# Singles in every odd step, small pieces of ScalarE and VectorE tied to the kind of step, and the output weights rounded on GpSimd

## The chip, the cores and the metric

The kernel runs on one core of one Trainium2 chip. The core has TensorE (matrix products, which go to the accumulation memory PSUM), VectorE, ScalarE and GpSimd, which run side by side and wait for each other by semaphores, and a sync engine, SP, that issues DMAs. The metric is device time of one execution in microseconds, median of the runs shown. The profile abbreviates: PE is TensorE, PEld its weight loads, DVE VectorE, ACT ScalarE, POOL GpSimd. L with a number is a line of the kernel; after a change the same code stands some lines further down.

## The reference

Two attention branches over the same input `x` (2048 rows of 512) are mixed by a gate per row; 32 heads of 16 in both.

```python
x = A_x
g = _sigmoid((x * gate_w).sum(-1, keepdims=True))
a = _A_ref(x, A_wqkv, A_wo)          # 8 keys per row: positions pos - 2*w, w = 0..7
b = _B_ref(x, B_wq, B_wk, B_wv, B_wo)  # all 2048 keys, one k and v for all heads
return g * a + (1 - g) * b
...
scores = jnp.einsum("bhqd,bkd->bhqk", q, k) * (Dh ** -0.5)
p = _softmax(scores, axis=-1)
o = jnp.einsum("bhqk,bkd->bhqd", p, v)
```

Branch A is small per row and runs mostly on GpSimd; branch B is the large one.

## The kernel before

**Front.** Up to about 278 us the projections of both branches run on TensorE (L1138), in float32 split into a rounded high part and a remainder. In between, maxima of branch B's first scores are taken. The change does not reorder anything there.

**Main loop.** Branch B is cut into 32 units `u` (four query blocks of 512 rows by eight groups of four heads) of 16 key blocks, so 512 steps `s`; step `s` is key block `s % 16` of unit `s // 16`. I number steps from 0. In a step TensorE does

- two score pairs (L488, `exp_pair`), each into one of two banks pairs `pe`, from which ScalarE takes an exponential of 128 x 1024 (L494);
- the weighted sum of the step before (L503, `weighted`) into `po`;
- work for a later unit: softmax needs each row's maximum before its exponentials, so scores are multiplied out once more in advance and reduced by VectorE. A *pair* fills two banks `pm` (L344) and costs VectorE one reduction of 128 x 1024 (L366, `fill_pair`); a *single* fills the bank `ps` and costs one of 128 x 512 (L378, `fill_one`). Each step takes a pair; some steps take a single as well.

Which steps take a single is decided by `singles(s)`: `owing` grows every step by the share of the remaining maxima that pairs cannot cover, a single is due when it reaches 1, and it is put off when VectorE is ahead of TensorE on the planner's clock.

**Small pieces.** Between steps stand short instructions for other work, all placed by the same planner, which keeps clocks `clk` for TensorE, ScalarE and VectorE, and `pool` for GpSimd, from estimated durations. `run_tasks` issues what is due by TensorE's clock: `shift_a` (ScalarE, tile `mh`, L458), which begins turning a unit's maxima into two more rows of its queries, and `finish_c` (VectorE, the transpose into `ob`, L543), which shapes two finished units. `run_pool` first runs the `hooks` that are due, `a_max` (VectorE, `amx`, L587), `a_exp` (ScalarE, `lg`, L596) and `a_sum` (VectorE, `asum`, L600), which are branch A's softmax; then it hands GpSimd pieces of branch A from the generator `work` as long as GpSimd's clock is less than 2.5 us ahead. A piece of GpSimd that needs a hook's result is held back until the hook has been issued. At the end of a unit (`kt == 0`) VectorE turns `po` (L517) and takes reciprocals (L523); when the last maximum of a unit is in, `filled` adds a reduction and a small transpose (`ms`, `mt`, L354 and L356).

**Output.** `work` also loads the output weights (`wo_load`, DMA on SP) and splits them (`wo_split`): ScalarE rounds 128 x 512 to `woh` (L81), GpSimd subtracts it for `wol` (L82). One such element of `extra` follows each pair of branch A's groups. After steps 271, 399 and 447 four output rows each are multiplied out in an *output phase* (`out_phase`, L821), in which score maxima go on; it needs the low halves that GpSimd subtracts in `prepare` (L662). Branch A has 32 groups, of which 16 belong to the first half of the rows and must be done before the first phase, the other 16 before the third. The last four output rows end the kernel.

All engines run their instructions in the order in which this program issues them, so the planner's placement is the order on each queue.

Of the kernel before, what the change touches and what calls it, by code (L numbers as in the profile page):

```python
# [48 lines left out]
def gated_mix_kernel(ctx, tc, xt, wa, wk, wq, wo_a, wo_b, out):  # L49
# [272 lines left out]
    hooks, pool, done = [], 0.0, set()  # L322

    marks, ups = [], [0]

    def mark(inst, end, up=None):
        marks.append((ups[0] if up is None else up, end, inst.ins.name))
# [21 lines left out]
    def filled(v, n):  # L349
        left[v] -= n  # L350
        if not left[v]:
            ms = wp.tile([P, 2, 2, 8], F32, name="ms")
            m = mx.pop(v).rearrange("p b i t k -> p b (i t) k")
            nc.vector.tensor_reduce(ms, m.unsqueeze(2).to_broadcast([P, 2, 2, 8, 4]), AX.X, ALU.max)  # L354
            mt = wp.tile([P, 32], F32, name="mt")
            nc.vector.transpose(mt, ms.rearrange("p b x y -> p (b x y)"))  # L356
            if v + 2 < NU:
                unit_tile(v + 2)
            tasks.append((after("dve", 0, 0.66) + (0.1 if pe else 2.0), shift_a, (v, mt)))
# [94 lines left out]
        fill_one(dst, key)  # L454

    def shift_a(v, mt):
        th = wp.tile([P, 32], F32R, name="mh")
        nc.scalar.activation(th, mt, AF.Identity, scale=mk[:, 4:5])  # L458
        at = after("act", 0, 0.25)
        ml = wp.tile([P, 32], F32R, name="ml")  # L460
        tasks.append((at + 0.1, shift_c, (v, mt, th, ml)))
# [74 lines left out]
                finish_c(u, obp["t"])  # L536

    def finish_c(u, t):
        shaped.add(u)
        qb, hg = divmod(u, NHG)  # L540
        if hg == 1:
            ob[qb] = pe[0].tile([P, C, 512], F32, name="ob", bufs=2)
        nc.vector.transpose(ob[qb][:, hg // 2, :], t.rearrange("p b h d -> p (b h d)"))  # L543
        after("dve", 0, 0.7)
        if qb == NQB - 1 and hg < NHG - 1:
            last_parts(hg // 2)
# [83 lines left out]
    p2b = []  # L630
# [18 lines left out]

    def wo_split(k, c):  # L650
        t = wot.pop((k, c))
        split(woh[k][:, c, :], wol[k][:, c, :], t, nc.gpsimd)

    turned, later = {}, {}

# [152 lines left out]

    def out_phase(js, n, s):

        m = 3 * (C + n)
        items = {}

        def mm(b, at):
            x, j, i = at
            if j not in items:
                items[j] = out_items(j, n)
                clk["pe"] = max(clk["pe"], free[f"e{x % 2}"])
            st, mv = items[j][i]
            h = slice(64 * b, 64 * b + 64)  # L820
            nc.tensor.matmul(eb[x % 2][:, b, :], st()[h], mv[h], start=(i == 0), stop=(i == m - 1))  # L821
            return T_R

        def done(at):
            x, j, i = at
            if i % 4 == 3:
                run_tasks()
                run_pool()
            if i == (5 if x else 1):
                turn(j, 1 - x % 2)  # L830
            if i == (8 if x else 6):
                later.pop(j)()
            if i == 3 * n and j != js[-1]:
                prepare(js[x + 1], n)
            if j == js[-1] and i > 9 and s not in exped and (free["e0"] <= clk["pe"] or i == m - 4):
                exp_pair(s, 0)
            if i == m - 1:
                out_store(j, x % 2, j == js[-1])

        stream([(x, j, i) for x, j in enumerate(js) for i in range(m)], mm, done, s)  # L840
# [47 lines left out]
    def singles(s):  # L888

        steps = 16 * (NU - 1) - 8 - s  # L890
        if steps <= 0 or to_go() <= 0:
            return to_go() > 0
        owing[0] += (to_go() - 1.94 * steps - 15.5 * (NJ - 4 - outs)) / steps
        owing[0] = min(owing[0], 3.0)
        if s % 16 == 1:
            return True
        if s % 16 == 0 or owing[0] < 1.0 or clk["dve"] - clk["pe"] > 1.5 and owing[0] < 2.0:
            return False
        return True

    def fill_ready(key, slack):
        if fillable() and free[key] <= clk["pe"] + slack:
# [104 lines left out]
    def work():  # L1007
# [28 lines left out]
        def load(i):  # L1036
            if i < len(order):
                yield lambda: order[i][0] // GC < ready_gg
                a_load(*order[i])
                yield 600 if i else 6200  # L1040

        order = [(g, hf) for hf in range(2) for g in range(NAG)]
        extra, summing = list(wos), []
        yield from load(0)
        yield from load(1)
        for i in range(0, len(order), 2):
            yield from a_scores(*order[i])
            hooks.append((pool + 3500, a_max, order[i][0], ("max",) + order[i]))
            for k, x in enumerate(a_scores(*order[i + 1])):
                yield x  # L1050
                if k == 6:
                    yield from sub(*order[i])
                if k == 11:
                    yield from sums()
            hooks.append((pool + 3500, a_max, order[i + 1][0], ("max",) + order[i + 1]))
            for k, x in enumerate(values(*order[i])):
                yield x
                if k == 6:
                    yield from sub(*order[i + 1])
                if k == 11:  # L1060
                    yield from sums()
            yield from load(i + 2)
            yield from values(*order[i + 1])
            yield from load(i + 3)
            if p2b and extra:
                for f, a in extra.pop(0):
                    f(*a)
                yield 1300
        assert not extra

    pieces, blocked = [work()], []
# [1 line left out]
    def run_pool():  # L1073
        nonlocal pool
        now = clk["pe"] * 1e3
        for h in sorted(hooks, key=lambda h: h[0]):
            if h[0] <= now:
                hooks.remove(h)
                h[1](h[2])
                done.add(h[3])  # L1080
        while pieces and pool < now + 2500:
            if blocked and not blocked[0]():
                break
            blocked.clear()
            x = next(pieces[0], None)
            if x is None:
                pieces.clear()
            elif callable(x):
                blocked.append(x)
            else:  # L1090
                pool = max(pool, now) + x
# [194 lines left out]
    qst.append(pe[0].tile([P, 2, 512], F32R, name="qsty"))  # L1286
    clear(NB + 1, nc.gpsimd)
    outs, due, led = 0, [], set()
    for s in range(NS + 1):
        u, kt = divmod(s, NJ)  # L1290
        if len(stacked) < NU and s >= max(2, 16 * (gone(len(stacked)) + 1)):
# [13 lines left out]
        if s - 1 in led:  # L1305
            order = (0, "m1", 1, "m2", "po")
        k, n = outs // 4, C - (outs >= NJ - 4)
        if outs == NJ - 4:
            if short > 0 and steps < 2:
                pause(short)  # L1310
# [12 lines left out]
        for which in order:  # L1323
            if which == "m2":
                if slots or half:
                    fill_ready("m2", 1.2 if s - 1 in led else M2S)
                else:
                    next(tail, None)
            elif which == "m1":
                if singles(s) and fill_ready("m1", M1S):  # L1330
                    owing[0] -= 1.0
            elif which == "po":
                weighted(s - 1)
            elif s < NS:
                exp_pair(s, which)
        if s - 1 in exped:
            weighted(s - 1)
            if kt == 0 and s < NS:
                finish_a(u - 1, nc.gpsimd)
        run_tasks()  # L1340
        run_pool()
    assert not slots and not half and not hooks and not tasks and first[0] > 12, (len(slots), len(hooks), len(tasks), outs)
# [78 lines left out]
```

## Time and profile before

| what | us |
|---|---|
| median of three runs (1441.04 to 1441.69) | 1441.46 |
| the profiled execution | 1441.69 |
| its span, first to last instruction | 1439.9 |
| TensorE busy | 1430.7 |
| ScalarE busy | 1299.8 |
| VectorE busy | 1120.1 |
| GpSimd busy | 946.9 |
| start of step 0 | 278.1 |
| the three output phases with their first step behind | 38.2, 38.7, 38.5 |

The time lies 1.8 us above the span, which is what surrounds the first and last instruction. The granted TensorE clock was 1.00. Busy time of TensorE says little by itself, since matmuls are pipelined and their ends modelled; starts of matmuls are the better ruler, and a step is measured from the start of its first score pair to that of the next step. In the timeline view a row has start, duration, engine, line, operation, output and inputs, count and, in brackets, how long the engine sat idle before it and for whom.

### The profile page before, as it was taken

The page shows a single profiled execution, that of the slowest core. Times are in us where ns is not written, and L with a number is a line of the kernel's source. Part 1 is how long each engine was busy: PE and PEld are TensorE (multiplying, and loading weights), DVE is VectorE, ACT ScalarE, POOL GpSimd, SP SyncE. Part 2 cuts the span into 40 slices and gives each one's busy share as a digit, 9 for nine tenths or more (in the row PEclk, how much of TensorE's full clock was granted, in tenths as well). Part 3 has the DMA queues.
Part 4 walks back from the last instruction along what each step waited for, and adds up shares of the span by engine and source line. Part 5 has one row for each costly group of instructions (what it writes and reads, how often), then busy time and mean ns, then how long its engine had stood idle before and what let it go on. Part 6 is the DMA issues. An engine that isn't in the chain of part 4 may idle for free.

```text
span 1439.9 us, 29642 instructions
## 1 busy us (share of the span) xinstructions
PE 1430.7 (99%) x10985; PEld 748.2 (52%) x10985; DVE 1120.1 (78%) x1851; ACT 1299.8 (90%) x1679; POOL 946.9 (66%) x1708
## 2 busy tenths in 40 slices
PE   9999999999999999999999999999999999999999
PEld 6999999833333333333333374333333743373335
DVE  7888899878787887887877777878778777777721
ACT  6888888799999999999999989999999889979994
POOL 6831989887889889888898898888883310140010
PEclk9999999999999999999999999999999999999999
DMA  7653342421211202012021120211200000000000
GB/s 237 179 165 111 114 135 74 129 64 39 80 43 49 79 13 79 32 39 69 13 80 45 40 88 18 81 43 43 72 12 13 17 16 1 2 31 2 1 2 30
DMA packets 45689, 85.51 MB, mean 59 GB/s; under 512 B 10400, under 2 KB 28376, under 8 KB 41448
## 3 DMA queue, kind: packets, MB, share of 16 engines
q1 hardware_dynamic: 38552, 45.21, 10.2%
q0 software_dynamic: 6560, 37.95, 8.1%
q8 instruction: 86, 1.41, 0.4%
q14 instruction: 59, 0.48, 0.1%
q10 hardware_dynamic: 432, 0.46, 0.1%
HBM read 57.77 MB, written 25.25 MB: 58 GB/s over the span
## 4 chain that ended last, share of the span: by engine, by line
PE 97%; ACT 1%; issue 1%; DMA 0%; DVE 0%; SPq 0%; ACTq 0%; DVEq 0%
PE po L503 35%; PE pe L488 24%; PE pf L1138 11%; PE pm L344 8%; PE ps L344 5%; PE pe L821 4%; PE pd L415 4%; PE po L344 1%; ACT pexp L494 1%; PE pf L344 1%; PE pe L1350 1%; PE pd L931 0%; DMA xraw<-xt 0%; PE pm L879 0%; PE pf L205 0%
## 5 line engine op out<-in xcount | busy, mean ns | idle before, releaser
L494 ACT ACTIVATE pexp<-pe 128x1024 f32<-128x1024 f32 x1021 | 982.6, 1023 | 51.6 <-PE pe L488 46.1
L366 DVE TENSOR_REDUCE mx<-pm 128x2 f32<-128x1024 f32 x479 | 585.2, 1222 | 193.7 <-PE pm L344 189.7
L503 PE MATMUL po<-pexp,vst 128*32 128x512 f32 x4096 | 545.5, 605 | 0.0
L488 PE MATMUL pe<-qst,kst 64*128 64x512 f32 x1914 | 477.1, 460 | 3.8 <-DVE other L704 3.2
L488 PEld LDWEIGHTS pe<-qst,kst 64*128 64x128 f32 x1914 | 185.5, 183 | 452.6 <-ACT pexp L494 413.4
L427 ACT ACTIVATE dd<-pd 128x512 f32<-128x512 f32 x410 | 231.7, 603 | 49.9 <-PE pd L415 39.6
L566 POOL TENSOR_TENSOR pr<-aext 128x256 f32<-128x256 f32 x256 | 182.0, 738 | 4.8 <-DMA aext<-ad 4.6
L344 PE MATMUL pm<-kst,qst 62*128 62x512 f32 x877 | 177.4, 397 | 0.0
L626 POOL TENSOR_TENSOR oa<-oa,av 128x256 f32<-128x256 f32 x224 | 164.1, 733 | 15.5
L378 DVE TENSOR_REDUCE mx<-ps 128x1 f32<-128x512 f32 x246 | 167.2, 680 | 2.6 <-PE pe L821 1.4
L503 PEld LDWEIGHTS po<-pexp,vst 128*32 128x32 f32 x4096 | 80.6, 108 | 158.4 <-issue 149.1
L415 PE MATMUL pd<-kd,qst 62*128 62x512 f32 x405 | 156.9, 395 | 0.0
L344 PE MATMUL ps<-kst,qst 62*128 62x512 f32 x387 | 154.6, 400 | 0.6 <-DVE mx L439 0.6
L623 POOL TENSOR_TENSOR av<-aext,lg 128x256 f32<-128x256 f32 x224 | 139.3, 622 | 13.0
L1138 PE MATMUL pf<-wah,xh 64*128 64x384 f32 (+1 forms) x496 | 144.1, 339 | 0.0
L1138 PE MATMUL pf<-wah,xl 64*128 64x384 f32 (+1 forms) x496 | 141.9, 338 | 0.0
L1138 PE MATMUL pf<-wal,xh 64*128 64x384 f32 (+1 forms) x496 | 141.8, 337 | 0.0
L439 DVE CUSTOM_DVE_ANT_0 dd<-ps,dd 128x512 f32<-128x512 f32 x164 | 113.0, 689 | 29.1 <-PE ps L344 12.4
L439 DVE CUSTOM_DVE_ANT_0 dd<-po,dd 128x512 f32<-128x512 f32 x146 | 100.5, 688 | 11.3 <-PE po L344 4.5
L530 POOL TENSOR_TENSOR rl<-rl,gate_t 128x16 f32<-128x16 f32 x31 | 7.1, 229 | 136.9 <-DVE rl L523 136.8
L1138 PEld LDWEIGHTS pf<-wah,xh 64*128 64x128 f32 x496 | 87.4, 186 | 0.4
L1138 PEld LDWEIGHTS pf<-wal,xh 64*128 64x128 f32 x496 | 87.0, 186 | 0.1
(224 smaller groups left out, 1909.3 us busy)
## 6 DMA issues: line engine op xcount, KB each, us to landing
aext<-ad POOLq DMA_DIRECT2D x32, 1056.0 KB, 5.4
ad<-stage SPq DMA_DIRECT2D x32, 384.0 KB
qst<-qd SPq DMA_DIRECT2D x60, 128.0 KB
xraw<-xt SPq DMA_DIRECT2D x16, 256.0 KB
qd<-qhi SPq DMA_DIRECT2D x16, 256.0 KB
qd<-qlo SPq DMA_DIRECT2D x16, 256.0 KB
qst<-qd SPq DMA_DIRECT2D x60, 64.0 KB
qst<-ml SPq DMA_DIRECT2D x212, 2.0 KB
```

The lines of the kernel that those rows point to most:

```text
L344: nc.tensor.matmul(dst, qst[place(v)][b:b + 62, pr, t * P:(t + 1) * P], kst[b:b + 62, kc * 512:(kc + 1) * 512], start=True, stop=True)
L366: got = nc.vector.tensor_reduce(m[:, :, pr, t, kc], dst, AX.X, ALU.max)
L378: got = nc.vector.tensor_reduce(m[:, odd, pr, t, kc:kc + 1], dst, AX.X, ALU.max)
L415: nc.tensor.matmul(dst, qst[place(v)][b:b + 62, pr, t * P:(t + 1) * P], kd[0][b:b + 62, kc // 2, :], start=True, stop=True)
L427: got = nc.scalar.activation(held[b][k], dst, AF.Relu)
L439: got = nc.vector.tensor_tensor_reduce(held[b][k], dst, held[b][k], 1.0, -FMAX, ALU.add, ALU.max, m[:, b, pr, t, kc:kc + 1])
L488: nc.tensor.matmul(bank[:, odd, :], kst[b:b + 64, kt * P:(kt + 1) * P], qst[place(u)][b:b + 64, pr, :], start=True, stop=True)
L494: got = nc.scalar.activation(e, bank, AF.Exp, scale=SCALE)
L503: nc.tensor.matmul(po[32 * i:32 * i + 32, :], vst[:, kt, :], pexp[s, i // 2][:, i % 2, :], start=(kt == 0), stop=(kt == NJ - 1))
L566: nc.gpsimd.tensor_mul(pr[:, k], q, e[:, o:o + NH, AC:2 * AC])
L626: nc.gpsimd.tensor_add(ao, ao, av)
L1138: inst = nc.tensor.matmul(home(x)[0][:, :n], l[h], r[h], start=(i == 0 and b == 0), stop=(i == 3 * C - 1 and b == 1))
```

## The change

Five edits go together.

1. `singles(s)`: from step 2 of a unit on, an odd step takes a single as long as `owing` is not negative; an even one only when 2 are owing. The first step of a unit takes none and its second always one, as before.
2. `calm(eng)`: in the main loop an engine may issue at most one small piece per step, and none where `quiet` is set. `quiet` is set behind every step: for ScalarE where the step had no single and the one before had, for VectorE where it had a single and the one before had none, and in any case at a unit's first step and where a unit's last maximum came in. A piece that finds its engine quiet is put back by half a microsecond or left in `hooks`.
3. `shift_a`, `finish_c` (but for the last units) and the hooks ask `calm`. In the output phases `main` is false, and nothing is held back there.
4. `wo_split` rounds on GpSimd instead of ScalarE.
5. The elements of `extra` are issued twice per pair of branch A's groups instead of once, and charge GpSimd 2000 ns instead of 1300.

```diff
+    quiet, main, over = {"act": 0, "dve": 0}, [False], []
+
+    def calm(eng):
+        if main[0] and quiet[eng] > 0:
+            return False
+        quiet[eng] = 1
+        return True
...
     def filled(v, n):
         left[v] -= n
         if not left[v]:
+            over.append(v)
...
     def shift_a(v, mt):
+        if not calm("act"):
+            tasks.append((clk["pe"] + 0.5, shift_a, (v, mt)))
+            return
...
     def finish_c(u, t):
+        if u < NU - NHG and not calm("dve"):
+            tasks.append((clk["pe"] + 0.5, finish_c, (u, t)))
+            return
...
     def wo_split(k, c):
         t = wot.pop((k, c))
-        split(woh[k][:, c, :], wol[k][:, c, :], t, nc.gpsimd)
+        nc.gpsimd.tensor_copy(woh[k][:, c, :], t)
+        nc.gpsimd.tensor_sub(wol[k][:, c, :], t, woh[k][:, c, :].bitcast(F32))
...
     def out_phase(js, n, s):
 
+        main[0] = False
...
         if s % 16 == 1:
             return True
-        if s % 16 == 0 or owing[0] < 1.0 or clk["dve"] - clk["pe"] > 1.5 and owing[0] < 2.0:
-            return False
-        return True
+        return s % 16 > 0 and owing[0] >= (0.0 if s % 2 else 2.0)
...
+        def outputs():
+            if p2b and extra:
+                for f, a in extra.pop(0):
+                    f(*a)
+                yield 2000
...
             yield from load(i + 2)
+            yield from outputs()
             yield from values(*order[i + 1])
             yield from load(i + 3)
-            if p2b and extra:
-                for f, a in extra.pop(0):
-                    f(*a)
-                yield 1300
+            yield from outputs()
...
-            if h[0] <= now:
+            if h[0] <= now and calm("act" if h[1] is a_exp else "dve"):
...
+    run, same = 0, 0
     for s in range(NS + 1):
...
+        main[0], lone = True, 0
...
                 if singles(s) and fill_ready("m1", M1S):
                     owing[0] -= 1.0
+                    lone = 1
...
+        run = run + 1 if lone == same else 1
+        same = lone
+        quiet["act"], quiet["dve"] = int(run < 2 and not lone), int(run < 2 and lone or kt == 0 or bool(over))
+        over.clear()
         run_tasks()
         run_pool()
```

TensorE's order over steps 127 to 129 (128 is the first of unit 8). `pe` are the banks of the exponentials, `pm` those of a pair, `ps` that of a single. Before:

```order
L488 MATMUL pe_4339<-qst_83,kst 128x512 x2
L344 MATMUL pm<-kst,qst_79 128x512 x2
L488 MATMUL pe_4340<-qst_83,kst 128x512 x2
L503 MATMUL po<-pexp,vst 32x512 x4
L488 MATMUL pe_4339<-qst_84,kst 128x512 x2
L344 MATMUL pm<-kst,qst_79 128x512 x2
L488 MATMUL pe_4340<-qst_84,kst 128x512 x2
L503 MATMUL po<-pexp,vst 32x512 x4
L488 MATMUL pe_4339<-qst_84,kst 128x512 x2
L344 MATMUL pm<-kst,qst_79 128x512 x2
L344 MATMUL ps<-kst,qst_79 128x512
L488 MATMUL pe_4340<-qst_84,kst 128x512 x2
```

and now:

```order
L500 MATMUL pe_4339<-qst_83,kst 128x512 x2
L352 MATMUL pm<-kst,qst_79 128x512 x2
L352 MATMUL ps<-kst,qst_79 128x512
L500 MATMUL pe_4340<-qst_83,kst 128x512 x2
L515 MATMUL po<-pexp,vst 32x512 x4
L500 MATMUL pe_4339<-qst_84,kst 128x512 x2
L352 MATMUL pm<-kst,qst_79 128x512 x2
L500 MATMUL pe_4340<-qst_84,kst 128x512 x2
L515 MATMUL po<-pexp,vst 32x512 x4
L500 MATMUL pe_4339<-qst_84,kst 128x512 x2
L352 MATMUL pm<-kst,qst_79 128x512 x2
L352 MATMUL ps<-kst,qst_79 128x512
```

Step 127 has a single (`ps`) now, and step 128 without one follows a step with one instead of a step without. Step 129 has its single in both.

ScalarE's order over steps 75 to 77, before (`woh` is a rounding of output weights, behind step 76):

```order
L494 ACTIVATE pexp<-pe_4339 128x1024
L494 ACTIVATE pexp<-pe_4340 128x1024
L494 ACTIVATE pexp<-pe_4339 128x1024
L494 ACTIVATE pexp<-pe_4340 128x1024
L81 ACTIVATE woh_4420<-os 128x512
L494 ACTIVATE pexp<-pe_4339 128x1024
L494 ACTIVATE pexp<-pe_4340 128x1024
```

and now (`lg` is an exponential of branch A, behind step 75, which has a single):

```order
L506 ACTIVATE pexp<-pe_4339 128x1024
L506 ACTIVATE pexp<-pe_4340 128x1024
L611 ACTIVATE lg<-lg 128x128
L506 ACTIVATE pexp<-pe_4339 128x1024
L506 ACTIVATE pexp<-pe_4340 128x1024
L506 ACTIVATE pexp<-pe_4339 128x1024
L506 ACTIVATE pexp<-pe_4340 128x1024
```

The rounding has left ScalarE. GpSimd has it now, ahead of its subtraction, for the first time here, between a load of branch A and its next products:

```order
L641 TENSOR_TENSOR oa<-oa,av 128x8x32
L570 DMA aext<-ad 128x2112
L667 CAST woh_4420<-os 128x512
L668 TENSOR_TENSOR wol_4421<-os,woh_4420 128x512
L581 TENSOR_TENSOR pr<-aext 128x256 x4
L587 TENSOR_TENSOR tr_4908<-pr 128x512
```

Before, only the subtraction stood on GpSimd.

GpSimd's order in the second output phase, from the low half of its first row (`qst<-ob`) to that of the third, before (`mx` is the clearing of a tile of maxima, `two` the sum of two halves of an output row, `rl` and `obp` a finished unit):

```order
L662 TENSOR_TENSOR qst_84<-ob,qst_84 128x512
L530 TENSOR_TENSOR rl<-rl,gate_t 128x16
L531 TENSOR_TENSOR obp<-tt,rl 128x16x16
L662 TENSOR_TENSOR qst_84<-ob,qst_84 128x512
L710 TENSOR_TENSOR two<-two 128x512
L338 MEMSET mx 128x64
L662 TENSOR_TENSOR qst_84<-ob,qst_84 128x512
```

and now, the ten rows that end with the low half of the third row:

```order
L631 TENSOR_TENSOR asum<-asum,gate 128x16
L632 TENSOR_TENSOR lg<-lg,asum 128x128
L638 TENSOR_TENSOR oa_4419<-aext,lg 128x8x32
L638 TENSOR_TENSOR av<-aext,lg 128x256
L726 TENSOR_TENSOR two<-two 128x512
L346 MEMSET mx 128x64
L641 TENSOR_TENSOR oa_4419<-oa_4419,av 128x8x32
L638 TENSOR_TENSOR av<-aext,lg 128x256
L641 TENSOR_TENSOR oa_4419<-oa_4419,av 128x8x32
L678 TENSOR_TENSOR qst_84<-ob,qst_84 128x512
```

Branch A's values (`av`, `oa`) and weights (`lg`, `asum`) stand between the low halves of the second and the third row now; before, branch A had ended ahead of this phase. The phases themselves follow the same steps as before.

## The prediction

> **What bounds the kernel now.** I read the page first, then the row of each stage, then single steps in order of time. The page's first part and its chain:
>
> ```profile
> PE 1430.7 (99%) x10985; PEld 748.2 (52%) x10985; DVE 1120.1 (78%) x1851; ACT 1299.8 (90%) x1679; POOL 946.9 (66%) x1708
> ...
> PE 97%; ACT 1%; issue 1%; DMA 0%; DVE 0%; SPq 0%; ACTq 0%; DVEq 0%
> ```
>
> TensorE carries nearly the whole chain, so a gain has to appear as a shorter stretch between TensorE instructions. The change touches only the 512 attention steps, of which 478 lie outside the three output phases. The windows view, cut at the starts of steps 2, 271, 274, 399, 402, 447, 450 and 489, with the exponentials of L494 alone (length, ScalarE busy, count; two exponentials are one step):
>
> ```profile
> 284.77:832.53 547.76, 517.07 (x538) 1.00 0.16 51
> 870.76:1124.08 253.32, 240.12 (x250) 1.00 0.12 39
> 1162.74:1253.62 90.88, 85.93 (x90) 1.00 0.02 4
> 1292.12:1371.27 79.15, 74.48 (x78) 1.00 0.02 5
> ```
>
> So 956/2 = 478 steps take 971.1 us. The same windows for the tile `ps` give the steps with a single (PE, PEld, DVE with the count of reductions); first and last of the four rows, the others count 60 and 21:
>
> ```profile
> 284.77:832.53 547.76, 54.05 (x136) 25.32 (x136) 92.20 (x137) 0.00 (x0) 1.00 0.16 51
> ...
> 1292.12:1371.27 79.15, 7.65 (x19) 3.53 (x19) 12.92 (x19) 0.00 (x0) 1.00 0.02 5
> ```
>
> 237 singles for 478 steps: half of the steps have one. What does an undisturbed alternation cost? In order of time, the first score matmul of step 184 and that of step 192, between which steps with and without a single alternate and no small piece of ScalarE or VectorE falls:
>
> ```profile
> 655.25 0.50 PE L488 MATMUL pe<-qsty,kst 64*128 64x512 f32 x2
> ...
> 671.31 0.50 PE L488 MATMUL pe<-qst,kst 64*128 64x512 f32 x2
> ```
>
> Eight steps in 16.06 us, 4.015 a pair. 239 such pairs would take 959.6, so 971.1 - 959.6 = 11.5 us of these stages is irregularity. That is the most that ordering can win, and the parts below say how much of it goes.
>
> **Part 1: two steps without a single in a row.** Steps 127 and 128 have none, step 129 has one (starts of steps 127, 128, 129 and 130, and a weight load between):
>
> ```profile
> 539.29 0.50 PE L488 MATMUL pe<-qst,kst 64*128 64x512 f32 x2
> ...
> 541.19 0.50 PE L488 MATMUL pe<-qst,kst 64*128 64x512 f32 x2
> ...
> 541.82 0.19 PEld L488 LDWEIGHTS pe<-qst,kst 64*128 64x128 f32 x2 [0.29 <-ACT pexp L494]
> ...
> 543.25 0.50 PE L488 MATMUL pe<-qst,kst 64*128 64x512 f32 x2
> ...
> 545.38 0.50 PE L488 MATMUL pe<-qst,kst 64*128 64x512 f32 x2
> ```
>
> The first takes 1.90 us, the second 2.06: its second score pair waits for ScalarE to leave bank `pe1`. The step with a single takes 2.13, which is TensorE's own time. So a step without a single is cheap only behind one with: the second in a row pays 0.16 and gets nothing for it. By the order of TensorE's instructions, before has 26 steps that follow another without a single, after has 4 (steps 347, 348, 383, 384). 22 x 0.16 = **3.5 us saved**. Runs of two with a single fall from 22 to 8; that their second step costs more no row quoted here shows, and I take nothing (up to 0.05 each would be 0.7, low end of the range). The planner ends with 239 steps with a single where it had 236: 3 x (2.13 - 1.90) = **0.7 us lost**.
>
> **Part 2: the eight roundings of the output weights leave ScalarE.** Four stand behind a step without a single, four behind one with. One of each (the rounding, then the starts of the steps after it, with a wait):
>
> ```profile
> 437.99 0.63 ACT L81 ACTIVATE woh<-os 128x512 fp32r<-128x512 f32 x1
> ...
> 439.64 0.50 PE L488 MATMUL pe<-qst,kst 64*128 64x512 f32 x2
> ...
> 440.50 0.19 PEld L488 LDWEIGHTS pe<-qst,kst 64*128 64x128 f32 x2 [0.56 <-ACT pexp L494]
> ...
> 441.93 0.50 PE L488 MATMUL pe<-qst,kst 64*128 64x512 f32 x2
> ```
>
> ```profile
> 496.38 0.50 PE L488 MATMUL pe<-qst,kst 64*128 64x512 f32 x2
> ...
> 496.62 0.63 ACT L81 ACTIVATE woh<-os 128x512 fp32r<-128x512 f32 x1
> ...
> 498.56 0.50 PE L488 MATMUL pe<-qst,kst 64*128 64x512 f32 x2
> ...
> 500.55 0.50 PE L488 MATMUL pe<-qst,kst 64*128 64x512 f32 x2
> ```
>
> In the first, the step from 439.64 takes 2.29 instead of 1.90: 0.39 lost, by a TensorE wait for ScalarE. In the second, 2.18 and 1.99 stand for 2.13 and 1.90: 0.14. Together 4 x 0.39 + 4 x 0.14 = **2.1 us saved**. GpSimd takes the casts over. The nearest row is its cast of a tile of the same shape, beside ScalarE's:
>
> ```profile
> L246 POOL CAST qhi<-qraw 128x512 fp32r<-128x512 f32 x13 | 7.9, 611 | 10.7 <-ACT qraw L239 10.7
> ...
> L81 ACT ACTIVATE woh<-os 128x512 fp32r<-128x512 f32 x8 | 5.1, 632 | 0.0
> ```
>
> 8 x 0.61 = 4.9 us more on GpSimd, behind which only its own later branch A pieces stand; what hides it is that no output phase needs them yet (rival C). The loads of the next weights on SP wait for GpSimd's subtraction of the one before, as they did; what is queued behind them on SP are loads of queries for units some steps ahead, so nothing is charged. The Trainium skill, page "Perfetto Trace Analysis", section "Optimizing GPSIMD Operations", says to prefer other engines, since GpSimd is generally slower; the two rows here are 611 against 632 ns, so for this operation the trace does not agree, and the rule would matter only by way of rival C.
>
> **Part 3: small pieces change their steps.** An exponential of branch A behind a step without a single, and the two step starts after it; then VectorE's transpose of `ob` behind a step with one:
>
> ```profile
> 698.58 0.31 ACT L596 ACTIVATE lg<-lg 128x128 f32<-128x128 f32 x1
> ...
> 700.23 0.50 PE L488 MATMUL pe<-qst,kst 64*128 64x512 f32 x2
> ...
> 702.19 0.51 PE L488 MATMUL pe<-qst,kst 64*128 64x512 f32 x2
> ```
>
> ```profile
> 358.54 0.70 DVE L543 STREAM_TRANSPOSE ob<-obp 128x512 f32<-128x512 f32 x1
> ...
> 360.05 0.50 PE L488 MATMUL pe<-qst,kst 64*128 64x512 f32 x2
> ...
> 360.41 0.19 PEld L344 LDWEIGHTS pm<-kst,qsty 62*128 62x128 f32 x2 [0.17 <-DVE mx L366]
> ...
> 362.31 0.50 PE L488 MATMUL pe<-qst,kst 64*128 64x512 f32 x2
> ```
>
> The first costs 1.96 - 1.90 = 0.06, two steps later, when the backlog reaches the bank. The second costs 2.26 - 2.13 = 0.13, because the pair reduction behind it comes late and TensorE waits for `pm`. Of 28 exponentials in these stages 15 stand behind a step without a single, and all but one of them move; 9 transposes stand behind a step with one and all move: 14 x 0.06 + 9 x 0.13 = **2.0 us saved**. In their new places I cost them at nothing: a step with a single gives ScalarE 2.13 - 1.90 = 0.23 more, nearly the 0.31 of a piece, and a step without has no second reduction on VectorE. If that cover is too thin, up to the whole 2.0 stays. The row maxima and reciprocals of branch A (a quarter to a third of a microsecond on VectorE) move too; they are taken at nothing, between -0.5 and +0.5. The new waits are only delays by the planner of at most a few steps; behind them are pieces of GpSimd.
>
> **Sum.** -3.5 + 0.7 - 2.1 - 2.0 = -6.9 us. This leaves 11.5 - 6.9 = 4.6 of irregularity: 4 x 0.16 are known, 0.7 are the added singles, and first steps behind output phases and ends of units remain. The profiled execution took 1441.69 with a span of 1439.9, so 1.8 lie around the span: 1441.69 - 6.9 = 1434.8. The median of the three runs is 0.2 below the profiled one: **1434.6**.
>
> **Rivals.** A: *ScalarE is the bound.* In the rows of the stages it is busy 94 to 95% with exponentials alone. Then regular singles buy nothing and the span loses just the 5.1 us of the `woh` row: 1436.4. Against it: the second step without a single waits for ScalarE, the first does not, and a step with a single is 0.23 longer although ScalarE does nothing more in it. The Trainium skill, "Perfetto Trace Analysis", "Identifying the Most-Contended Engine", says that TensorE's busy share is no measure and that for ScalarE occupancy is; it would point to A, and the step rows speak against it for the alternation.
>
> B: *the pieces only move their lateness.* Parts 1 and 2 hold, part 3 gives nothing: 1441.5 - 3.5 - 2.1 + 0.7 = 1436.6. For it: 0.31 is more than 0.23.
>
> C, the slow side: *GpSimd comes late.* With delays and casts, branch A's last two groups slip from before the second output phase into it. There the `lo` halves of the rows are subtracted on GpSimd with 9 to 12 branch A instructions between them; at the 0.6 to 0.75 us of such an instruction some 7 to 8 us. A row of the phase takes 38.66/4 = 9.7 us and the subtraction is issued half a row ahead, so if a whole group stood ahead of it TensorE would wait up to 3.5 us in each of three rows, and the exponentials of branch A that now fall into the phase (0.31 each) come on top: +11, 1445.6. It decides the sign once more than 6.9 are lost there. The first two output phases (windows; PE, PEld, DVE, ACT, POOL):
>
> ```profile
> 832.53:870.76 38.23, 37.24 (x332) 31.11 (x329) 29.25 (x76) 30.52 (x51) 35.16 (x50) 1.00 0.27 90
> 1124.08:1162.74 38.66, 37.64 (x333) 29.62 (x329) 28.93 (x75) 30.27 (x50) 13.97 (x18) 1.00 0.07 22
> ```
>
> Against it: the first phase already runs with GpSimd 92% busy in branch A and is the shorter one.
>
> D: *no change.* The pieces held back delay GpSimd and VectorE until new waits eat the gain: 1441. Against it: the order shows the alternation really built, with the same three phases at the same steps.
>
> **Chances.** Forecast 0.64, B 0.14, A 0.09, D 0.07, C 0.06. The range reaches down towards the 11.5 of all irregularity (1430.0) and up past A and B with 1 us for the second output phase: 1431.0 to 1438.0, which leaves out C and D. About 0.2% (2.9 us) can be told from no change: faster (below 1438.6) 0.87, within 0.07, slower 0.06.
>
> **What would show it.** The four stages should fall from 971.1 to about 964 us, with steps alternating 1.90 and 2.13; no L81 row of `woh` on ScalarE and a cast near 0.61 on GpSimd; the second phase between 38 and 39.5 with GpSimd near 90%. I am wrong if steps without a single, behind one with, often take more than 1.95, if the second phase passes 42, or if the gain is ScalarE's 5 us and no more.

## The result, and the profile after

The changed kernel takes 1433.12 us (median of five runs, 1432.92 to 1433.91) where the kernel before took 1441.04 (1440.89 to 1441.69) beside it. The ratio is 0.9944, with a 95% interval of 0.9931 to 0.9957: faster by 0.56%. The forecast was 1434.6 in a range of 1431.0 to 1438.0. The profiled execution took 1432.93 us with a span of 1431.2, against 1441.69 and 1439.9.

The page of the changed kernel, busy times and the engines' shares of the chain:

```profile
PE 1422.7 (99%) x10985; PEld 750.6 (52%) x10985; DVE 1121.1 (78%) x1854; ACT 1296.0 (91%) x1671; POOL 949.3 (66%) x1708
...
PE 97%; POOL 2%; ACT 0%; issue 0%; DVE 0%; POOLq 0%; ACTq 0%; DVEq 0%
```

TensorE carries 97% of the chain as before. Its busy time fell by 8.0, about as much as the span (8.7), although it issues the same 10985 matmuls: modelled busy time swallows the short waits, which is why the stages have to be read by starts of steps.

The windows of the four stages between the output phases, with ScalarE's exponentials (now L506; length, ScalarE busy, count), and the first and the last row for the tile `ps` (PE, PEld, DVE with the count of reductions; the two others count 60 and 22):

```profile
284.26:825.91 541.65, 515.25 (x538) 1.00 0.15 47
864.34:1115.68 251.34, 239.09 (x250) 1.00 0.15 48
1154.16:1244.87 90.71, 85.75 (x90) 1.00 0.02 4
1283.47:1362.49 79.02, 74.35 (x78) 1.00 0.02 5
```

```profile
284.26:825.91 541.65, 53.59 (x136) 25.37 (x136) 92.59 (x137) 0.00 (x0) 1.00 0.15 47
...
1283.47:1362.49 79.02, 8.37 (x21) 3.90 (x21) 14.24 (x21) 0.00 (x0) 1.00 0.02 5
```

The same 478 steps take 962.7 us instead of 971.1: 8.4 of the 8.7 us of span were won here. 239 steps in them have a single, as the order had it (the reductions count 240, since one at the edge of a window belongs to the step ahead). The other 0.3 are the front, whose program is the same and which ended 0.5 earlier in this execution, and the phases and the end, 0.2 longer in sum.

The place where the order was shown, steps 126 to 129 in order of time (starts of their first score pairs):

```profile
534.18 0.50 PE L500 MATMUL pe<-qst,kst 64*128 64x512 f32 x2
...
536.08 0.49 PE L500 MATMUL pe<-qst,kst 64*128 64x512 f32 x2
...
538.20 0.50 PE L500 MATMUL pe<-qst,kst 64*128 64x512 f32 x2
...
540.10 0.50 PE L500 MATMUL pe<-qst,kst 64*128 64x512 f32 x2
```

1.90, 2.12, 1.90: step 128, which took 2.06 before, is now a cheap step behind one with a single. An exponential of branch A in its new place, behind the step that starts at 692.81 and has a single, and the three steps after it:

```profile
692.81 0.50 PE L500 MATMUL pe<-qst,kst 64*128 64x512 f32 x2
...
694.95 0.50 PE L500 MATMUL pe<-qst,kst 64*128 64x512 f32 x2
695.18 0.31 ACT L611 ACTIVATE lg<-lg 128x128 f32<-128x128 f32 x1
...
696.84 0.50 PE L500 MATMUL pe<-qst,kst 64*128 64x512 f32 x2
...
698.97 0.50 PE L500 MATMUL pe<-qst,kst 64*128 64x512 f32 x2
...
700.87 0.50 PE L500 MATMUL pe<-qst,kst 64*128 64x512 f32 x2
```

1.89, 2.13 and 1.90 follow: it costs nothing. The first two output phases (PE, PEld, DVE, ACT, POOL) and GpSimd's new rounding among the groups of instructions:

```profile
825.91:864.34 38.43, 37.43 (x333) 31.33 (x329) 29.56 (x78) 30.81 (x51) 35.62 (x52) 1.00 0.29 89
1115.68:1154.16 38.48, 37.19 (x329) 30.40 (x326) 28.59 (x76) 29.72 (x50) 33.82 (x57) 1.00 0.06 22
```

```profile
L667 POOL CAST woh<-os 128x512 fp32r<-128x512 f32 x8 | 5.0, 624 | 0.0
```

Branch A did slip into the second phase: GpSimd is busy 33.8 of its 38.5 us, 14.0 before. The phase is no longer for it (38.66 before). The 2% of GpSimd in the chain come from these phases, but no engine's wait for GpSimd's low halves lengthened them.

To compare kernels step by step I hold each step outside the phases against 1.893 us without and 2.128 with a single, its undisturbed lengths. What stands above that, the *excess*, was 10.8 us before and is 1.7 after. It is laid to the piece or pattern that stands in the step or up to two steps ahead.

| excess in the four stages, us | before | after |
|---|---|---|
| second or third step without a single in a row | 4.0 (26 places) | 0.35 (4) |
| second or third step with a single in a row | 1.1 (22) | 0.2 (8) |
| rounding `woh` on ScalarE | 1.95 (8) | none |
| small pieces (`lg`, `ob`, `amx`, `mh`) and first steps behind something else | 3.4 (29) | 0.8 (4) |

The rows add up to 10.4 and 1.4; the rest is spread over undisturbed steps. The four places that are left are the first steps behind the three phases, 0.16 each, and step 18 behind the first end of a unit, 0.35. The prediction's first sign of being wrong was that steps without a single, behind one with, often take more than 1.95 us; of 235 these four do.

### The profile page after: what moved, and what is told of

Its sections match the earlier page's. It is cut to its first block, busy times and chain, and to the rows that moved or that the text cites. A ratio compares the mean times of both kernels' runs of the same rounds, so it can differ in the third digit from the quotient of the medians.

```text
span 1431.2 us, 29647 instructions
## 1 busy us (share of the span) xinstructions
PE 1422.7 (99%) x10985; PEld 750.6 (52%) x10985; DVE 1121.1 (78%) x1854; ACT 1296.0 (91%) x1671; POOL 949.3 (66%) x1708
## 4 chain that ended last, share of the span: by engine, by line
PE 97%; POOL 2%; ACT 0%; issue 0%; DVE 0%; POOLq 0%; ACTq 0%; DVEq 0%
PE po L515 36%; PE pe L500 24%; PE pf L1157 11%; PE pm L352 8%; PE ps L352 5%; PE pd L424 4%; PE pe L838 3%; PE po L352 1%; PE pe L1376 1%; PE pf L352 1%; PE pd L946 0%; POOL oa L641 0%; PE pf L205 0%; POOL pr L581 0%; POOL two L726 0%; POOL qst L678 0%
## 5 line engine op out<-in xcount | busy, mean ns | idle before, releaser
L506 ACT ACTIVATE pexp<-pe 128x1024 f32<-128x1024 f32 x1021 | 980.2, 1022 | 47.3 <-PE pe L500 45.7
L500 PE MATMUL pe<-qst,kst 64*128 64x512 f32 x1914 | 470.5, 458 | 3.6 <-DVE other L720 3.5
L500 PEld LDWEIGHTS pe<-qst,kst 64*128 64x128 f32 x1914 | 181.0, 183 | 452.0 <-ACT pexp L506 402.8
```

What stands on the lines that cost most here:

```text
L500: nc.tensor.matmul(bank[:, odd, :], kst[b:b + 64, kt * P:(kt + 1) * P], qst[place(u)][b:b + 64, pr, :], start=True, stop=True)
L506: got = nc.scalar.activation(e, bank, AF.Exp, scale=SCALE)
```

## The experiments

The theory was the prediction's: TensorE's order decides, a step without a single is cheap only behind one with, and a small piece costs what its step cannot cover. Rivals were A, that ScalarE is the bound, and B, that moved pieces only move their lateness. The times are medians, each ratio is to the kernel before on the same chip, with its 95% interval.

| kernel | us | ratio |
|---|---|---|
| the change | 1433.12 | 0.9944 (0.9931 to 0.9957) |
| singles_only | 1436.70 | 0.9969 (0.9956 to 0.9981) |
| round_only | 1439.22 | 0.9986 (0.9977 to 0.9995) |
| no_round | 1434.23 | 0.9952 (0.9939 to 0.9964) |
| no_calm | 1435.16 | 0.9958 (0.9945 to 0.9972) |
| old_singles | 1436.39 | 0.9966 (0.9953 to 0.9978) |
| act_behind_single | 1433.64 | 0.9943 (0.9929 to 0.9958) |
| act_behind_none | 1436.94 | 0.9967 (0.9954 to 0.9980) |
| dve_behind_single | 1447.42 | 1.0041 (1.0026 to 1.0056) |
| dve_behind_none | 1435.72 | 0.9958 (0.9942 to 0.9975) |
| full_pairs | 1433.18 | 0.9944 (0.9931 to 0.9958) |
| pool_more | 1448.90 | 1.0045 (1.0028 to 1.0062) |
| pool_charged | 1433.40 | 0.9944 (0.9928 to 0.9961) |

### Parts alone, and the change without one part

**singles_only**: the kernel before with the new rule of `singles(s)` and nothing else.

```diff
-        if s % 16 == 0 or owing[0] < 1.0 or clk["dve"] - clk["pe"] > 1.5 and owing[0] < 2.0:
-            return False
-        return True
+        return s % 16 > 0 and owing[0] >= (0.0 if s % 2 else 2.0)
```

> The kernel before with the new rule for singles alone; pieces are placed as before and the output weights are rounded on ScalarE. By its order 16 steps without a single still follow another such step (before 26, after 4), and 234 steps have a single (before 236 by the same count). My steps: 10 x 0.16 less for the runs, some 0.5 less for singles, so about 2 us below the kernel before, 1439.0. If ScalarE were the bound (rival A), which has the same work here, no change: 1441.0.

It gained 4.4 us, more than was expected. Two things were missing. The runs of steps with a single cost something: 22 second or third steps 1.1 us before, 4 of them 0.1 here. And the 16 steps that still follow another without a single stand in runs of three, and a run of three pays once (1.5 us in all for 16 steps, not 16 x 0.16 = 2.6). It also ended with 231 singles where the kernel before has 236, worth 1.2 (two fewer were expected).

**old_singles**: the change with the old rule, the same diff backwards.

> The changed kernel with the rule for singles of the kernel before; pieces are still held back by kind of step and the rounding stays on GpSimd. Its order has 23 steps without a single that follow another one without (the changed kernel 4) and 22 second steps with a single (8). My steps: 19 x 0.15 = 2.9 for the former, up to 14 x 0.05 = 0.7 for the latter: 3.0 to 3.6 above the changed kernel, 1436.4. Rival A (ScalarE is the bound, so regular singles buy nothing): 1433.1.

As expected. 23 steps follow another without a single here and cost 3.9 us, 0.17 each; 22 second steps of two with a single cost 1.4. ScalarE has the same 1671 instructions as in the changed kernel, and yet 3.3 us are gone: A falls.

**round_only**: the kernel before with the roundings on GpSimd. **no_round**: the change with them on ScalarE.

```diff
-        split(woh[k][:, c, :], wol[k][:, c, :], t, nc.gpsimd)
+        nc.gpsimd.tensor_copy(woh[k][:, c, :], t)
+        nc.gpsimd.tensor_sub(wol[k][:, c, :], t, woh[k][:, c, :].bitcast(F32))
```

> The kernel before with the rounding of the output weights on GpSimd alone, at the same places in its program. My steps: 4 x 0.39 + 4 x 0.14 = 2.1 us less, 1438.9. Rival A: the whole 5.1 us of ScalarE, 1435.9. If GpSimd's later pieces were waited for: no gain or a loss, 1441 or more.

> The changed kernel with the rounding of the output weights put back on ScalarE. Its order has six roundings behind a step with a single and two behind one without. My steps: 6 x 0.14 + 2 x 0.39 = 1.6 us more than the changed kernel, 1434.7. Rival A: 5.1 more, 1438.2.

1.9 us gained by the part alone and 1.1 lost without it. In the regular order the price depends on the step again. Step 56 of no_round has no single and a rounding behind it (starts of steps 57, 58 and 59):

```profile
395.67 0.50 PE L500 MATMUL pe<-qst,kst 64*128 64x512 f32 x2
396.13 0.63 ACT L81 ACTIVATE woh<-os 128x512 fp32r<-128x512 f32 x1
...
397.80 0.50 PE L500 MATMUL pe<-qst,kst 64*128 64x512 f32 x2
...
400.07 0.50 PE L500 MATMUL pe<-qst,kst 64*128 64x512 f32 x2
```

Step 58 takes 2.27 instead of 1.89, the second step behind the piece. So do both of this kind (0.39 each); the six behind a step with a single pay 0.155 each. That makes 1.7, and 1.6 was expected; the 1.1 of the medians is less. In the profiled executions the stages are 1.5 longer than in the change and the second phase is 0.3 shorter (38.19); why is not known.

**no_calm**: the change with `calm` never refusing.

```diff
     def calm(eng):
-        if main[0] and quiet[eng] > 0:
+        if False:
             return False
```

> The changed kernel in which no small piece is ever held back; the rule for singles and the rounding on GpSimd stay. Its order has 16 runs of two without a single (the changed kernel 4), 9 branch A exponentials and 4 shifts behind a step without a single (1 and none). My steps: 12 x 0.16 = 1.9 for the runs, 0.8 for ScalarE's pieces and about 1 for VectorE's behind steps with a single: 3.5 to 4 us more, 1437. Rival B (the pieces only move their lateness): 1.9 more at most, 1435.0 or below.

It lost 2.0 us. The time alone decides little, since B allowed 1.9; the steps decide. Nine exponentials `lg` stand behind a step without a single again and pay 0.07 each two steps later, ten transposes `ob` behind one with and pay 0.156: 2.2 us, which moving the pieces wins, and the second phase takes 38.87. So B falls for these two. Less was lost than expected because the planner came to 231 singles instead of 239, worth 1.9, and gave about 1.1 of it back in runs of three steps without one.

### The price of a small piece, measured by itself

Four kernels add 59 equal instructions to the changed kernel, one in every eight steps, whose results are not read: a ScalarE copy of 128 x 128 behind a step with a single (`s % 8 == 3`) or without (`== 6`), and a VectorE reduction in the same places.

```diff
+        if 16 < s < 488 and s % 8 == 3 and main[0] and order:
+            nc.scalar.activation(junk, ident, AF.Copy)
```

> The changed kernel with 59 added copies of a 128x128 tile on ScalarE (about 0.31 us each), whose result nobody reads, one in every eighth step: 58 behind a step with a single, one behind a step without. Everything else is issued in the same order. My steps: the slack behind a step with a single hides them, 0 to 0.02 each, 1433 to 1434.5. Rival A (ScalarE is the bound): 59 x 0.31 = 18 more, 1451. Rival B (a piece only moves its lateness): 0.06 each, 1436.7.

> The same 59 copies on ScalarE, all behind a step without a single. My steps: 0.06 to 0.07 each, two steps later, 1436.7 to 1437.3. Rival A: 1451. If the place did not matter: the same time as with the copies behind steps with a single.

> The changed kernel with 59 added reductions of 640 elements a partition on VectorE (about 0.7 us each), whose result nobody reads: 58 behind a step with a single. My steps: 0.12 each, as the transposes of ob cost there before, 1440. If VectorE has room everywhere (it is busy 78%): 1433.

> The same 59 reductions on VectorE, all behind a step without a single. My steps: 0.01 each, 1433 to 1434. If the place did not matter: as with the reductions behind steps with a single.

The first of them among the groups of instructions (count, busy, mean ns); the other three read 311, 812 and 799 ns:

```profile
L1370 ACT ACTIVATE junk<-ident 128x128 f32<-128x128 f32 x59 | 18.4, 312 | 0.0
```

18.4 us more of ScalarE behind steps with a single cost 0.5 us or nothing. That is the end of A: with ScalarE the bound, all 18.4 would show. B, by which each copy would cost 0.06 here too (1436.7), falls with it. The Trainium skill, page "Perfetto Trace Analysis", section "Identifying the Most-Contended Engine", takes occupancy as the measure for ScalarE, and by it this engine (95% in the stages) would come first; the 18.4 us that cost 0.5 do not agree with that here.

The same copies behind steps without a single cost 3.8 us. In act_behind_none, one of them, starts of steps 190 to 193 and TensorE's wait:

```profile
664.12 0.50 PE L501 MATMUL pe<-qsty,kst 64*128 64x512 f32 x2
...
666.00 0.50 PE L501 MATMUL pe<-qsty,kst 64*128 64x512 f32 x2
...
666.48 0.31 ACT L1370 ACTIVATE junk<-ident 128x128 f32<-128x128 f32 x1
...
668.13 0.50 PE L501 MATMUL pe<-qst,kst 64*128 64x512 f32 x2
...
668.67 0.18 PEld L501 LDWEIGHTS pe<-qst,kst 64*128 64x128 f32 x2 [0.24 <-ACT pexp L507]
...
670.10 0.50 PE L501 MATMUL pe<-qst,kst 64*128 64x512 f32 x2
```

The copy belongs to the step from 664.12. The next step is undisturbed (2.13), the one after it waits for ScalarE to leave the second bank pair and takes 1.97 instead of 1.89. Over all such places the price is 0.07, and it comes two steps later.

VectorE missed in both places. Behind a step with a single a reduction cost 0.24 instead of 0.12. In dve_behind_single (the step from 682.36 is the second behind the reduction's own, VectorE's pair reduction is L376, the weight load of the pair L353):

```profile
680.84 0.81 DVE L1370 TENSOR_REDUCE junk<-ident 128x5 f32<-128x640 f32 x1
...
681.56 1.22 DVE L376 TENSOR_REDUCE mx<-pm 128x2 f32<-128x1024 f32 x1
...
682.36 0.50 PE L501 MATMUL pe<-qst,kst 64*128 64x512 f32 x2
682.83 0.19 PEld L353 LDWEIGHTS pm<-kst,qst 62*128 62x128 f32 x2 [0.29 <-DVE mx L376]
...
684.71 0.75 PE L501 MATMUL pe<-qst,kst 64*128 64x512 f32 x3
```

The pair reduction of 681.56 is late by the added piece, and the next pair may not overwrite `pm` before it ends: the step from 682.36 takes 2.35 instead of 2.13.

Behind steps without a single the 59 reductions cost 2.6 us where 0.01 each, 0.6 in all, was expected. The mean of 0.04 stands at no place. Three of them run into an output phase; of the 56 others 46 cost nothing, and ten cost 0.26 each: those that share their step with a transpose `ob`, so that VectorE has 0.70 and 0.78 to do behind one step. In dve_behind_none, one of them (both pieces belong to step 38; the starts of steps 40 and 41, and TensorE's wait):

```profile
358.64 0.70 DVE L559 STREAM_TRANSPOSE ob<-obp 128x512 f32<-128x512 f32 x1
...
359.27 0.78 DVE L1370 TENSOR_REDUCE junk<-ident 128x5 f32<-128x640 f32 x1
...
360.76 0.49 PE L501 MATMUL pe<-qst,kst 64*128 64x512 f32 x2
...
361.23 0.19 PEld L353 LDWEIGHTS pm<-kst,qsty 62*128 62x128 f32 x2 [0.29 <-DVE mx L376]
...
362.88 0.50 PE L501 MATMUL pe<-qst,kst 64*128 64x512 f32 x2
```

Step 40 takes 2.12 instead of 1.89, by the same wait for `pm`. The added pieces never asked `calm`, which would have kept the two apart.

The prices fit one form, length less a cover, and nothing below the cover:

| engine, behind a step | lengths and prices, us | cover worked out from them |
|---|---|---|
| ScalarE, without a single | 0.31: 0.07; 0.63: 0.39 | 0.24 |
| ScalarE, with a single | 0.31: 0.01; 0.63: 0.155 | 0.47 |
| VectorE, with a single | 0.70: 0.13; 0.81: 0.24 | 0.57 |
| VectorE, without a single | 0.70: 0.01; 0.81: 0; 0.70 and 0.78 together: 0.26 | 1.22 |

(0.63 is the rounding in no_round, 0.70 the transpose `ob` before and after the change.) ScalarE's two covers differ by 0.23, the length that a single adds to a step; VectorE's differ by 0.65, close to the 0.68 of the reduction that a single brings. Each cover rests on one or two lengths above it; others were not tried.

### Can singles be saved as well?

**full_pairs**: the change, but a pair is always taken whole, and a leftover half waits for the next single.

```diff
-            elif half and (not slots or half[0][0] < slots[0][0] or slots[0][0] >= len(stacked)):
+            elif half and not (slots and slots[0][0] < len(stacked) and stacked[slots[0][0]] <= clk["pe"]):
```

> The changed kernel in which the pair of a step is always a whole one: a half left over at a unit's end waits for the next single instead of taking the place of a pair (11 steps in the changed kernel). By its order 10 steps fewer have a single, 20 steps without a single follow another one without (4) and 4 second steps with a single are left (8). My steps: 10 x 0.235 = 2.4 less, 16 x 0.09 to 0.15 = 1.4 to 2.4 more, 0.1 less: 1432.0 to 1433.0. If singles were only TensorE time, with no price on two steps without one in a row: 1430.7.

No gain, and 0.2 above the range expected: ten singles fewer (229) are worth 2.35 us, and what they leave open gives it back: 20 steps that follow another without a single cost 1.8, where the change has 4 for 0.35, and small pieces the rest. They stand in runs of three; one of them, step starts:

```profile
1034.23 0.50 PE L500 MATMUL pe<-qst,kst 64*128 64x512 f32 x2
...
1036.13 0.50 PE L500 MATMUL pe<-qst,kst 64*128 64x512 f32 x2
...
1038.20 0.50 PE L500 MATMUL pe<-qst,kst 64*128 64x512 f32 x2
...
1040.10 0.50 PE L500 MATMUL pe<-qst,kst 64*128 64x512 f32 x2
...
1042.23 0.50 PE L500 MATMUL pe<-qst,kst 64*128 64x512 f32 x2
```

1.90, 2.07, 1.90, then 2.13 with a single. The second step pays and the third does not, in this run and in the others.

### How much room GpSimd has

**pool_more**: each of GpSimd's eight roundings is issued nine times, 64 x 0.62 = 40 us more. Only the last one's value counts.

```diff
-        nc.gpsimd.tensor_copy(woh[k][:, c, :], t)
+        for _ in range(9):
+            nc.gpsimd.tensor_copy(woh[k][:, c, :], t)
```

> The changed kernel in which GpSimd rounds each of the eight tiles of output weights nine times instead of once: 64 x 0.62 = 40 us more on GpSimd, all before the first output phase; the order of every engine is otherwise that of the changed kernel. My steps: GpSimd is idle for more than that in the first stage and its pieces are not due before the phases, so 1433 to 1434.5. Rival C (TensorE or ScalarE waits for GpSimd's later pieces): waits of ScalarE and VectorE for branch A's products in the first stage, 1440 or more.

This was wrong by 15 us: 1448.9. The output phases kept their length (38.46 the first, 38.48 the second). The stages took 979.1, 16.4 more than in the change, and 14 of that in six steps. Rows of the view of waits (us in total, times, longest):

```profile
PEld pm L352 <- DVE mx L375: 11.9, 9, 3.2
...
DVE amx L602 <- POOL lg L595: 8.7, 3, 3.8
```

And the costliest place in order of time, step 132 to 133:

```profile
555.71 0.49 PE L500 MATMUL pe<-qst,kst 64*128 64x512 f32 x2
...
557.51 0.37 DVE L602 TENSOR_REDUCE amx<-lg 128x16 f32<-128x128 f32 x1 [3.81 <-POOL lg L595]
557.80 1.22 DVE L375 TENSOR_REDUCE mx<-pm 128x2 f32<-128x1024 f32 x1
...
559.07 0.80 PE L352 MATMUL pm<-kst,qst 62*128 62x512 f32 x2 [2.86 <-DVE mx L375]
...
562.09 0.79 PE L500 MATMUL pe<-qst,kst 64*128 64x512 f32 x2
```

VectorE has been given branch A's row maximum `amx` at the time the planner's clock says GpSimd is done. GpSimd is late by its burst, VectorE waits for it 3.81 us in order, the pair reduction stands behind it, and TensorE behind that. The step takes 6.4 us.

That leaves two readings: the planner's clock did not know of the 40 us, or GpSimd has no 40 us to give. **pool_charged** issues the same casts and charges them.

```diff
-                for f, a in extra.pop(0):
+                more = extra.pop(0)
+                for f, a in more:
                     f(*a)
-                yield 2000
+                yield 2000 + 5000 * sum(f is wo_split for f, a in more)
```

> The changed kernel with each GpSimd rounding issued nine times, as in pool_more (1448.9), but with 5000 ns more charged to GpSimd's clock in the planner behind each of the eight bursts, so that the due times of branch A's small pieces on VectorE and ScalarE move back with them. Only the value of the last cast is read. Theory 1 (in pool_more the time went because VectorE and ScalarE were given pieces whose operands GpSimd had not yet made, and everything behind such a piece waited in order): nearly all of the 15.8 us comes back, 1433 to 1437, and the steps of 3 to 6 us in the stages are gone; branch A runs later, up to 40 us of its work nearer to the third output phase. Theory 2 (GpSimd has no 40 us to give, or the bursts themselves hold up TensorE): 1444 or more, with lost time that is as large but elsewhere.

1433.4: all of it came back. The steps of 3 to 6 us and the waits of `amx` for `lg` are gone. Windows of the first stage in pool_charged and in pool_more, and of the second phase in pool_charged (PE, PEld, DVE, ACT, POOL):

```profile
284.67:826.34 541.67, 541.67 (x3896) 203.99 (x3896) 437.59 (x498) 520.19 (x564) 452.57 (x845) 1.00 0.15 47
...
1116.09:1155.64 39.55, 38.32 (x338) 31.63 (x335) 30.55 (x83) 32.42 (x54) 35.54 (x53) 1.00 0.23 77
```

```profile
284.24:842.42 558.18, 547.98 (x3896) 205.48 (x3897) 438.03 (x501) 521.59 (x566) 469.29 (x878) 0.99 0.14 46
```

In the first stage GpSimd is busy 452.6 of 541.7 us, 21 more than the 431.4 in the change, and the stage is as long as there. The second phase is 1.1 us longer; the stages end 0.6 shorter. Branch A's work moved back instead, above all into the third stage, where GpSimd is busy 47.5 us instead of 16.5. So GpSimd has the room; the 40 us fitted into the first stage with part of branch A moved behind it. The planner also came to 233 singles, six fewer, which is worth 1.4, and to 14 steps that follow another without one, which cost 1.35 where the change's 4 cost 0.35, so the 0.3 us are not the price of the casts alone. What cost 15.5 us was that the program was ordered by a clock that did not know of the work.

## Why the prediction was right, point by point

**The bound** held. The gain is where the prediction put it, in the 478 steps, by shorter stretches between TensorE's starts; ScalarE's 18.4 us more at no price, and old_singles' 3.3 us at equal ScalarE work, show that TensorE's order decides and not ScalarE's sum.

**Part 1** was -3.5 + 0.7. The second and third steps without a single fell from 4.0 us to 0.35, so -3.65, and three singles more are the 0.7 (the 237 of the prediction's first reading counts one reduction of the step ahead of a window; TensorE's column adds up to 236, which its sum used). The premise that each such step costs 0.16 is right for runs of two, which is what before has; in runs of three it is paid once. Runs with a single were taken at nothing with 0.7 as the end of the range; they gave 0.9. A view of the kernel before shows why they cost: in 20 of the 22 second or third steps TensorE waits some 0.2 us for VectorE to leave `ps`, the bank of the single before; in the row of step 260 (810.66, L344) it is 0.23, and the step takes 2.19 instead of 2.13.

**Part 2** was -2.1 and is -1.95 by the trace; round_only gained 1.9. GpSimd's cast took 0.624 where 0.61 was priced, and nothing waited for it.

**Part 3** was -2.0. By the table small pieces gave 2.6. About 2.0 of it is what was priced: before, 15 `lg` behind a step without a single paid 0.05 each two steps later, 0.8 in all, and nine `ob` behind one with 0.13 each, 1.1; in their new places 24 `lg` cost 0.02 and 13 `ob` 0.1 in sum. Taking the new places at nothing was right, but the reason given, that a step with a single gives ScalarE 0.23 and that this is nearly enough, was not. The cover there is 0.47, since the 0.24 behind a step without counts as well. For VectorE the reason given, no second reduction, fits the two covers.

**The sum.** -6.9 was forecast and -8.4 came in the stages. The miss of 1.5 is 0.9 in the runs of two with a single, which the prediction took at nothing, and 0.6 in part 3, where the pieces other than `lg` and `ob` (`amx`, `mh`, ends of units) were taken at nothing; parts 1 and 2 were off by 0.15 in opposite directions. Nothing in the mechanism had to be changed for it. Between the profiled executions the gain is 8.8; between the medians it is 7.9, since the one of before was 0.65 above its median and the one of after 0.2 below. The range held A (1436.4) and B (1436.6) too, so that the time lies in it says little for the mechanism; the stages, forecast at 964 and measured at 962.7, and the runs above say more.

**Rivals.** A fell as above, and B for `lg` and `ob`. C's load arrived as it was described, with GpSimd at 88% of the second phase, and cost nothing; pool_charged puts 35.5 us on GpSimd there and takes 1.1 more for a phase with more maxima in it, so the 3.5 us a row were far off. In what condition C would bite in a phase was not tried; in pool_more a late GpSimd did bite, in the stages and by way of VectorE. D is excluded by the interval.

## What to carry to other kernels

Where engines alternate at nearly equal loads, price a small piece by the step that it stands behind: its length less that step's cover, which one kernel with some 60 dummies measures, if they are read place by place: the mean of dve_behind_none hid 46 free places and ten dear ones. Here this was worth more than the engine's share of busy time, which named the wrong engine. And before putting more on an engine with idle time in a planned, in-order program, tell the planner: 40 us on GpSimd cost 0.3 us where they were charged and 15.8 where they weren't.

## What the runs showed of the hardware

Lateness shows after its cause: two steps later for the added pieces of ScalarE (0.07 behind a step without a single), for those of VectorE (0.26, behind a step without a single only at the ten places) and for the roundings of no_round (0.39 and 0.155). The piece's own step and the next are longer by 0.01 at most, in the mean. A long step's own pieces are the wrong place to look for why it is long.

The second step without a single in a row mostly pays 0.16 to 0.18 and a third nothing. That ScalarE then sets an even pace explains it only in part: its exponentials take 1.92 us a step (515.25 for 538), two steps at that pace 3.84, and the first two steps of the run in full_pairs take 3.97. Why the third pays nothing stays open.

A wait of TensorE of some 3 us costs more than itself. In pool_more around step 132 the windows, cut where the record of the clock changes, give the granted clock (the first of the last three numbers):

```profile
555.00:558.62 3.62, 1.21 (x10) 0.19 (x2) 1.11 (x2) 2.10 (x3) 3.38 (x13) 1.00 0.38 103
558.62:565.44 6.82, 6.37 (x27) 2.06 (x27) 4.04 (x5) 3.22 (x4) 6.58 (x12) 0.50 0.03 6
565.44:570.00 4.56, 4.56 (x35) 1.76 (x33) 3.43 (x4) 3.78 (x5) 4.25 (x7) 1.00 0.01 2
```

In a wait of 2.86 us, which ends at 559.07, the clock falls to 0.50 and stays there for 6.8 us; a pair of matmuls takes 0.80 instead of 0.40, and steps 132 and 133 lose 6.0 us together for that one wait. The wait of 2.75 us in step 100 was followed by 3.4 us at 0.50 (490.35 to 493.76), the one of 2.02 in step 74 by none. The Trainium skill, "TensorE: Matmul & The Clock Gate", section "HAM oscillation — how this bites in real kernels", asks for no idle gap of TensorE over about 3.4 us; here 2.75 and 2.86 were enough.
